# A gated MLP's first layer with seven products of parts for eight, over pairs of token blocks, on one Trainium2 core

## The chip, the core and the metric

The kernel runs on one core of a Trainium2 chip. The core has a matrix engine (TensorE, here PE), a vector engine (VectorE, DVE), an engine for activations and copies (ScalarE, ACT), a general engine (GpSimd, POOL) and a queue that issues the transfers (SyncE, SP). Only PE multiplies matrices; its results land in PSUM, eight banks of 2 KB per partition, from which DVE and ACT can read, and POOL can't in this kernel. Everything else lies in SBUF or in DRAM. The metric is the device time of one execution in microseconds (us); lower is better.

## What is computed

Decay attention over 4 batches of 8 heads, 576 positions and 64 dimensions; its output, 2304 tokens of 512 features, goes through a leaky MLP and then through a gated MLP. All in fp32:

```python
def _moe_ref(x, w_in, w_out, alpha):            # d_ff 2048
    h = x @ w_in
    g = np.maximum(h, 0.0) + alpha * np.minimum(h, 0.0)
    return (g @ w_out).astype(np.float32)

def _moe2_ref(x, w_a, w_b, w_out):              # d_ff 1536
    a = x @ w_a
    b = x @ w_b
    return (a * b @ w_out).astype(np.float32)

def reference(**kwargs):
    ...
    x = np.ascontiguousarray(attn_out.transpose(0, 2, 1, 3)).reshape(B * S, H * D)
    x = _moe_ref(x=x, **moe_kwargs)
    return _moe2_ref(x=x, **moe2_kwargs)
```

## The kernel before

**Split products.** Each fp32 number is held as a high part (rounded to the matrix engine's fp32r) and a low part, the rest. A product of two such numbers is three matmuls, high by high, high by low, low by high (`mm3`, L643 to L646). An operand that was computed is split by a cast on ACT (high) and a subtraction on POOL (low).

**Weights.** `weight` (L115 to L133) loads 512 KB by SP's queue (L123), rounds it in one ACT operation (L127) and three DVE operations (L129 to L131), casts it on ACT (L132) and subtracts on POOL (L133).

**Stages.** Attention runs up to some 366 us, with the first MLP's part a (inner blocks 0 to 6 of 16, `mlp1a`) between its steps; the rest of part a follows up to 427 us. Meanwhile the weights of inner blocks 7 to 11 are prepared, ten of them (L786 to L793). Then come two passes (L847 to L868) over six blocks of 384 tokens, with inner blocks 7 to 11 and 12 to 15: 12 matmuls for the hidden part `hb`, leaky on ACT and DVE, split on ACT and POOL (`gb`), and two inner blocks later 12 matmuls for `ya` (`passes_out`, L821 to L845). At a block's end DVE adds the running sum `yl`, loaded from DRAM. In the second pass the sum is split (`yhl`) and both parts are stored. While the passes run, weights of the next inner blocks and of the second MLP are prepared at a pace of 0.8 per inner block (L861).

**Second MLP** (L877 to L915). All its weights are resident in the end. Six token blocks of 384, twelve inner blocks each:

```python
for o, w in ((aps, W["a", fi]), (bps, W["b", fi])):
    for c in range(C):
        mm3(o[:, :n], w[:, 0, c], w[:, 1, c], yh[:, c, :n], yl[:, c, :n], c == 0, c == C - 1)
...
act.copy(asb[:, :n], aps[:, :n])
dve.tensor_tensor(asb[:, :n], bps[:, :n], asb[:, :n], op=ALU.mult)
```

That is 24 matmuls of 384 columns for `a` and `b`, a copy on ACT, the multiplication on DVE, the split into `gg`, and two inner blocks later nine matmuls of 512 columns for the output `o` (`second2`, L884), whose three banks collect all twelve inner blocks. Products rotate through four PSUM banks (`pst`, "mm"), sums through four others (`psa`, "acc"). The next block's two tiles (768 KB each) are loaded while a block runs (`load_pair`).

**What sets the order.** A framework schedules every engine's instructions by its own model of their times, from the order in which the code is written, buffer pools and priorities. Each engine then works through a fixed list; an instruction that must wait holds what stands behind it. SP's queue is such a list too.

## Time and profile before

| | |
|---|---|
| three runs | 1119.04, 1121.77, 1122.03 us, median 1121.77 |
| profiled execution | 1120.79 us, its span from first to last instruction 1119.0 us |
| mean granted clock of PE | 0.995 |
| busy share of the span | PE 95%, DVE 48%, ACT 45%, POOL 43% |
| moved by DMA | 141.18 MB, mean 126 GB/s |
| chain of work that ended last | PE 60%, DVE 4%, DMA 2%, POOL 2%, ACT 1% |

The first line is what a user sees; the profile tells of one execution only. Busy shares are means over the whole span. The chain of work that ended last is followed back from the last instruction, at each step to what released it. A wait is put down to the releaser that came last.

### The profile page before, as it was taken

Reading aid. Unit: us, or ns where it says so; the run is one execution under the profiler, and the core shown is the slowest. Engines: PE = TensorE matmul, PEld = TensorE weight load, DVE = VectorE, ACT = ScalarE, POOL = GpSimd, SP = SyncE. Lnnn points to the kernel's source line nnn. Section 1 sums busy time; section 2 is a strip of 40 time slices with the busy share of each in tenths; the row PEclk is TensorE's granted clock in tenths of the full one; section 3 lists DMA queues with packets and bytes.
Section 4 is the critical chain, followed back from the end, with each engine's and each line's share of the span. In section 5 each row is a group of like instructions: output and inputs, shape, how many; then the busy total and the mean of one; then the engine's idle time right before and its main releaser. Section 6 shows DMA issues by size and latency. Waiting matters only on the chain.

```text
span 1119.0 us, 18298 instructions
## 1 busy us (share of the span) xinstructions
PE 1064.5 (95%) x6663; PEld 1000.2 (89%) x6663; DVE 540.8 (48%) x1156; ACT 507.4 (45%) x1271; POOL 481.0 (43%) x559
## 2 busy tenths in 40 slices
PE   5989989898899998999998999999999999999997
PEld 3768988888898988999998999999999999999996
DVE  4666988888888286776577345300000000000000
ACT  5777767777677464555455543321121111111211
POOL 5445766666577355465467654311111111111111
PEclk9999999999999999999999999999999999999999
DMA  5546576776864856787778973120100100200000
GB/s 111 150 113 185 111 142 129 181 140 122 205 136 89 237 179 202 223 267 235 252 246 297 294 244 110 41 85 1 54 32 1 57 29 1 86 1 1 29 1 28
DMA packets 206093, 141.18 MB, mean 126 GB/s; under 512 B 137332, under 2 KB 195700, under 8 KB 206004
## 3 DMA queue, kind: packets, MB, share of 16 engines
q1 hardware_dynamic: 206004, 140.03, 45.0%
q8 instruction: 52, 0.85, 0.3%
q14 instruction: 37, 0.30, 0.1%
HBM read 88.30 MB, written 33.65 MB: 109 GB/s over the span
## 4 chain that ended last, share of the span: by engine, by line
PE 60%; DVE 4%; DMA 2%; POOL 2%; ACT 1%; issue 1%; SPq 0%; DVEq 0%; ACTq 0%; POOLq 0%
PE a L646 5%; PE a L645 5%; PE b L646 5%; PE b L645 5%; PE b L644 5%; PE a L644 5%; PE o L644 4%; PE o L645 4%; PE o L646 4%; PE ya L645 3%; PE ya L646 3%; PE ya L644 3%; PE hb L644 3%; PE hb L646 3%; PE hb L645 3%; DMA wr_in<-in_moe_w_in 1%
## 5 line engine op out<-in xcount | busy, mean ns | idle before, releaser
L910 DVE TENSOR_TENSOR as<-b,as 128x384 f32<-128x384 f32 x72 | 40.1, 557 | 366.4 <-PE b L646 366.4
L912 POOL TENSOR_TENSOR gg<-as,gg 128x384 fp32r<-128x384 f32 x72 | 73.7, 1023 | 330.8 <-ACT gg L911 330.8
L909 ACT COPY as<-a 128x384 f32<-128x384 f32 x72 | 34.6, 480 | 172.0 <-PE a L646 172.0
L911 ACT CAST gg<-as 128x384 fp32r<-128x384 f32 x72 | 36.9, 513 | 149.6 <-DVE as L910 149.6
L639 DVE SCALAR_TENSOR_TENSOR lt<-lu,nal,lt 128x288 f32<-128x288 f32 (+1 forms) x110 | 77.1, 701 | 52.0 <-ACT lt L638 51.6
L646 PE MATMUL a<-yh,w_a 128*128 128x384 f32 x288 | 97.2, 338 | 0.0
L646 PE MATMUL b<-yh,w_b 128*128 128x384 f32 x288 | 97.1, 337 | 0.0
L645 PE MATMUL a<-yl,w_a 128*128 128x384 f32 x288 | 97.1, 337 | 0.0
L644 PE MATMUL b<-yh,w_b 128*128 128x384 f32 x288 | 97.1, 337 | 0.0
L645 PE MATMUL b<-yl,w_b 128*128 128x384 f32 x288 | 97.1, 337 | 0.0
L644 PE MATMUL a<-yh,w_a 128*128 128x384 f32 x288 | 97.1, 337 | 0.0
L644 PE MATMUL o<-w_o,gg 128*128 128x512 f32 x216 | 84.4, 391 | 0.0
L645 PE MATMUL o<-w_o,gg 128*128 128x512 f32 x216 | 84.4, 391 | 0.0
L646 PE MATMUL o<-w_o,gg 128*128 128x512 f32 x216 | 84.2, 391 | 0.0
L355 ACT ACTIVATE s<-s,nm 128x512 f32<-128x512 f32 (+3 forms) x128 | 71.6, 560 | 15.3 <-DVE nm L354 14.1
L645 PE MATMUL ya<-gb,w_out 128*128 128x384 f32 x216 | 73.5, 340 | 1.6 <-POOL gb L641 1.6
L641 POOL TENSOR_TENSOR gb<-lt,gb 128x384 fp32r<-128x384 f32 x54 | 61.4, 1140 | 29.3 <-ACT gb L640 26.7
L646 PE MATMUL ya<-gb,w_out 128*128 128x384 f32 x216 | 73.0, 338 | 0.0
L644 PE MATMUL ya<-gb,w_out 128*128 128x384 f32 x216 | 70.7, 339 | 1.8 <-DVE yl L837 1.8
L645 PE MATMUL y<-g,w_out 128*128 128x288 f32 x224 | 66.8, 304 | 3.2 <-POOL g L641 3.0
L644 PE MATMUL h<-xh,w_in 128*128 128x288 f32 x224 | 67.3, 303 | 2.3 <-ACT lt L638 2.2
L644 PE MATMUL y<-g,w_out 128*128 128x288 f32 x224 | 65.5, 306 | 3.0 <-ACT lt L638 1.9
(185 smaller groups left out, 3150.1 us busy)
## 6 DMA issues: line engine op xcount, KB each, us to landing
yl<-ya_d SPq DMA_DIRECT2D x48, 192.0 KB
wr_in<-in_moe_w_in SPq DMA_DIRECT2D x16, 512.0 KB
wr_out<-in_moe_w_out SPq DMA_DIRECT2D x16, 512.0 KB
wr_a<-in_moe_w_a SPq DMA_DIRECT2D x12, 512.0 KB
wr_b<-in_moe_w_b SPq DMA_DIRECT2D x12, 512.0 KB
wr_o<-in_moe_w_out SPq DMA_DIRECT2D x12, 512.0 KB
qkn<-in_q SPq DMA_DIRECT2D x64, 72.0 KB
qkn<-in_k SPq DMA_DIRECT2D x64, 72.0 KB
```

The source lines that it names most:

```text
L355: act.activation(s, s, AF.Exp, bias=nm, scale=-1.0, accum_out=sm)
L639: dve.scalar_tensor_tensor(t, u, nal[:, fi:fi + 1], t, op0=ALU.mult, op1=ALU.add)
L641: pool.tensor_tensor(gl, t, f32(gh), op=ALU.subtract)
L644: pe.matmul(o, lh, rh, start=start, stop=False)
L645: pe.matmul(o, lh, rl, start=False, stop=False)
L646: pe.matmul(o, ll, rh, start=False, stop=stop)
L909: act.copy(asb[:, :n], aps[:, :n])
L910: dve.tensor_tensor(asb[:, :n], bps[:, :n], asb[:, :n], op=ALU.mult)
L911: ap_["last"] = act.copy(g[:, 0, :n], asb[:, :n]).ins
L912: pool.tensor_tensor(g[:, 1, :n], asb[:, :n], f32(g[:, 0, :n]), op=ALU.subtract)
```

## The change

The second MLP's first layer works on a pair of token blocks at once. Two token blocks (rows 1 and 2) by two halves of the 512 features (columns 1 and 2) make a 2 x 2 matrix of parts, and so do the halves of `w_a` and `w_b`. The 2 x 2 product of these takes eight products of parts; Strassen's scheme in Winograd's form takes seven, of sums of parts. A product of parts is six matmuls of 384 columns, so a pair and an inner block take 42 instead of 48.

- The sums of token parts (`pair_parts`) are made on DVE when a pair's second block leaves the second pass, and seven split tiles per pair go to DRAM: 14 `put`s a pair (a cast on ACT, a subtraction on POOL, one store), 4 behind the even and 10 behind the odd block, where there were 4 behind each block.
- `weight` for kind "b" makes four sums of weight halves on DVE and keeps five parts ("h") instead of `w_b`, with three casts and three subtractions.
- The sums of products are made on DVE, straight from PSUM.
- The twelve inner blocks are taken in three groups of four; each group goes over the three pairs (0 1 2, 2 1 0, 0 1 2), so there are 36 slots. A group's output sums go through DRAM (`po_d`): copied by ACT in the first group, added by DVE in the second and third. Weights of the next groups are loaded and prepared in the slots that `when` names.
- Seven tiles of 768 KB make a pair; `load_y` loads the next pair's tiles one by one behind the products of a turn's last slot (`leaves`), into eight buffers.
- The second layer's nine matmuls (`unit`) come twice in a slot.
- Weights in the passes come at 0.4 per inner block; the staging pool of the weights is taken ahead of the pool of x tiles; in the second pass the running sums are loaded one inner block later; at the program's start two fills move from POOL to DVE; three output buffers instead of two.

```diff
 def weight(kind, i, p, after=None):
+    x = rounded(kind, i, after)
+    if kind == "b":
+        xa = ap_["xa"]
+        s = mp["stage"].tile([128, 8, 128], F32, tag="ws", name=f"ws_{i}", bufs=1)
+        t = W["h", i] = p.tile([128, 2, 10, 128], F32R, tag="h", name=f"w_h{i}")
+        dve.tensor_tensor(s[:, 0:2], x[:, 0:2], xa[:, 0:2], op=ALU.subtract)
+        dve.tensor_tensor(s[:, 2:4], x[:, 2:4], s[:, 0:2], op=ALU.subtract)
+        dve.tensor_tensor(s[:, 4:6], x[:, 2:4], x[:, 0:2], op=ALU.subtract)
+        dve.tensor_tensor(s[:, 6:8], xa[:, 2:4], s[:, 2:4], op=ALU.subtract)
+        parts(t, slice(0, 2), x[:, 2:4])
+        parts(t, slice(2, 6), s[:, 0:4])
+        parts(t, slice(6, 10), s[:, 4:8])
+        return
...
+        dve.memset(ones, 1.0)
         for i in range(2):
...
-            fill(t[64:], 0.0)
+            dve.memset(t[64:], 0.0)
...
-            if i == 0:
-                fill(ones, 1.0)
...
+        mp["stage"] = lpool(right, "wstage2", 2, "right")
+        mp["wx"] = 3
         xp = lpool(right, "xb", 2, "right")
-        mp["stage"] = lpool(right, "wstage2", 2, "right"), C
...
-            if fi < f0 + 2:
+            if fi in (f0 + p, f0 + p + 1):
...
+        def pair_parts(blk, e, ya):
+            pair, odd = divmod(blk, 2)
+            def put(x, j, c):
+                yh = yp.tile([128, 2, TB], F32R, tag="yhl", name=f"yhl_{pair}_{j}_{c}")
+                act.copy(yh[:, 0], x)
+                pool.tensor_tensor(yh[:, 1], x, f32(yh[:, 0]), op=ALU.subtract)
+                sp.dma_start(f32(yq_d)[:, pair, j, c::2], f32(yh))
+            if not odd:
+                kept[e] = ya[e]
+                put(ya[e], 0 if e < 2 else 3, e % 2)
+            elif e >= 2:
+                c = e - 2
+                a11, a12, a21, a22 = kept[c], kept[e], ya[c], ya[e]
+                s1 = yp.tile([128, TB], F32, tag="s1", name=f"s1_{pair}_{c}", bufs=2)
+                dve.tensor_tensor(s1, a21, a22, op=ALU.add)
+                put(s1, 2, c)
...
+        visits = [0, 1, 2, 1, 0, 1, 2]
+        def load_y():
...
-                due += 0.8
+                due += 0.4
...
-        op_ = lpool(left, "os", 2)
+        op_ = lpool(left, "os", 3)
...
+            for t in range(nt):
+                acc, o = open_o[t], open_o[nt + t]
+                if g_:
+                    dve.tensor_tensor(o, acc, o, op=ALU.add)
+                else:
+                    act.copy(o, acc)
+                r0 = t0 + t * 128
+                sp.dma_start(out[r0:r0 + 128, :] if g_ == NG - 1 else po_d[g_ % 2][:, r0 // 128], o)
...
+            def both(pl, x, y, o, blk):
+                g = pl.tile([128, 2, TB], F32R, tag="g", name=f"gg_{s_}_{blk}")
+                dve.tensor_tensor(o, x, y, op=ALU.mult)
+                ap_["last"] = act.copy(g[:, 0], o).ins
+                pool.tensor_tensor(g[:, 1], o, f32(g[:, 0]), op=ALU.subtract)
+                return g
...
+            def product(j, w, c0):
+                o, y = pst.tile([128, 512], F32, tag="mm", name=f"p{j}_{s_}")[:, :TB], Y[7 * v_ + j]
+                for c in range(2):
+                    mm3(o, w[:, 0, c0 + c], w[:, 1, c0 + c], y[:, c], y[:, 2 + c], c == 0, c == 1)
+                if leaves:
+                    load_y()
+                return o
...
+            p1 = product(0, wa_, 0)
+            act.copy(ta, p1)
+            p6 = product(1, wh_, 4)
+            add(td, p6, ta)
+            p5 = product(2, wh_, 2)
+            add(tb, p5, td)
+            p2 = product(3, wa_, 2)
+            add(ta, p2, ta)
+            next_weight()
+            p3 = product(4, wh_, 0)
+            add(tc_, p3, tb)
+            ga = both(ga_, ta, tc_, tc_, 0)
+            unit(s_)
+            next_weight()
+            p7 = product(5, wh_, 6)
+            add(tb, p7, tb)
+            add(td, p7, td)
+            unit(s_)
+            next_weight()
+            p4 = product(6, wh_, 8)
+            add(td, p4, td)
+            gb = both(gp_, td, tb, td, 1)
```

**PE in the second MLP.** Before, in the third token block: `a` and `b` of inner block 4 (twelve matmuls each, three shown), then nine for the output.

```order
L644 MATMUL a_768_4_9700<-yh_768_9012,w_a4_7105 128x384 [waits Activation_49]
L645 MATMUL a_768_4_9700<-yl_768_9013,w_a4_7105 128x384
L646 MATMUL a_768_4_9700<-yh_768_9012,w_a4_7105 128x384
...
L644 MATMUL b_768_4_9701<-yh_768_9012,w_b4_7156 128x384 [waits DVE_49]
L645 MATMUL b_768_4_9701<-yl_768_9013,w_b4_7156 128x384
L646 MATMUL b_768_4_9701<-yh_768_9012,w_b4_7156 128x384
...
L644 MATMUL o_768_0_9647<-w_o2_6876,gg_768_2_9641 128x512 [waits Activation_49]
...
L644 MATMUL o_768_1_9648<-w_o2_6876,gg_768_2_9641 128x512
...
L644 MATMUL a_768_5_9741<-yh_768_9012,w_a5_7369 128x384 [waits Activation_49]
```

After, in slot 16, the first slot of a turn and group (the first matmul of each run shown; `p0` to `p6` are the products, `yq` the tiles, `o_1_...` the second layer of the turn before).

```order
L675 MATMUL p0_16_10061<-yq_21_9153,w_a4_9299 128x384 [waits DMAHW7_49,DVE_49]
...
L675 MATMUL p1_16_10069<-yq_22_9951,w_h4_9331 128x384 [waits DMAHW0_49,DVE_49]
...
L675 MATMUL p2_16_10077<-yq_23_9961,w_h4_9331 128x384 [waits DMAHW1_49,DVE_49]
...
L675 MATMUL o_1_1536_0_9916<-w_o7_9829,gg_15_0_10004 128x512 [waits Activation_49]
...
L675 MATMUL p3_16_10085<-yq_24_9971,w_a4_9299 128x384 [waits DMAHW2_49,DVE_49]
...
L675 MATMUL p4_16_10093<-yq_25_9981,w_h4_9331 128x384 [waits DMAHW4_49,Activation_49]
...
L675 MATMUL o_1_1920_0_10129<-w_o4_8700,gg_12_1_9711 128x512
...
L675 MATMUL p5_16_10120<-yq_26_10001,w_h4_9331 128x384 [waits DMAHW5_49,DVE_49]
...
L675 MATMUL o_1_1920_0_10129<-w_o5_8893,gg_13_1_9840 128x512
...
L675 MATMUL p6_16_10141<-yq_27_10024,w_h4_9331 128x384 [waits DMAHW6_49]
```

Seven runs of six matmuls stand where 48 stood, each with its own tile, and the second layer's matmuls stand between them.

**POOL where the second pass ends.** Before: the last `gb`, four splits of the running sum (`yhl`), the first `gg`.

```order
L641 TENSOR_TENSOR gb_1920_15_8338<-lt_15_8339,gb_1920_15_8338 128x384 [waits PE_49,Activation_49]
L843 TENSOR_TENSOR yhl_1920_0_8387<-yl_1_1920_0_8309,yhl_1920_0_8387 128x384 [waits DMAHW2_49,DMAHW4_49,Activation_49,Pool_49]
L843 TENSOR_TENSOR yhl_1920_1_8393<-yl_1_1920_1_8311,yhl_1920_1_8393 128x384 [waits DMAHW3_49,DMAHW0_49,Activation_49]
L843 TENSOR_TENSOR yhl_1920_2_8399<-yl_1_1920_2_8346,yhl_1920_2_8399 128x384 [waits DMAHW5_49,DMAHW2_49,Activation_49]
L843 TENSOR_TENSOR yhl_1920_3_8405<-yl_1_1920_3_8348,yhl_1920_3_8405 128x384 [waits DMAHW6_49,DMAHW4_49,Activation_49]
L912 TENSOR_TENSOR gg_0_0_8461<-as_0_0_8462,gg_0_0_8461 128x384 [waits Activation_49]
L133 TENSOR_TENSOR w_b8_8425<-wx_b8_0_8428,w_b8_8425 128x512 [waits Activation_49]
```

After, `yhl_2_...` being the last pair's puts (pair, product, half) and `w_h2` the parts of weight b of inner block 2:

```order
L1016 TENSOR_TENSOR gg_0_0_8426<-tc_0_8365,gg_0_0_8426 128x384 [waits Activation_49]
L882 TENSOR_TENSOR yhl_2_2_0_8305<-s1_2_0_8303,yhl_2_2_0_8305 128x384 [waits DMAHW0_49,Activation_49]
L882 TENSOR_TENSOR yhl_2_5_0_8310<-yl_1_1920_0_8254,yhl_2_5_0_8310 128x384 [waits DMAHW1_49,Activation_49]
L882 TENSOR_TENSOR yhl_2_1_0_8315<-yl_1_1536_0_8086,yhl_2_1_0_8315 128x384 [waits DMAHW2_49,Activation_49]
L1016 TENSOR_TENSOR gg_0_1_8457<-td_0_8366,gg_0_1_8457 128x384 [waits PE_49,Activation_49]
L882 TENSOR_TENSOR yhl_2_6_0_8319<-yl_1_1920_2_8272,yhl_2_6_0_8319 128x384 [waits DMAHW3_49,Activation_49]
L882 TENSOR_TENSOR yhl_2_4_0_8324<-yl_1_1536_2_8123,yhl_2_4_0_8324 128x384 [waits DMAHW4_49,Activation_49]
L140 TENSOR_TENSOR w_a3_8437<-wx_a3_8432,w_a3_8437 128x512 [waits Activation_49]
L882 TENSOR_TENSOR yhl_2_2_1_8331<-s1_2_1_8329,yhl_2_2_1_8331 128x384 [waits DMAHW5_49,Activation_49]
...
L1016 TENSOR_TENSOR gg_1_0_8524<-tc_1_8463,gg_1_0_8524 128x384 [waits Activation_49]
...
L1016 TENSOR_TENSOR gg_1_1_8567<-td_1_8464,gg_1_1_8567 128x384 [waits PE_49,Activation_49]
...
L140 TENSOR_TENSOR w_h2_8407<-wx_b2_8401,w_h2_8407 128x256 [waits Activation_49]
```

Puts of the last pair now stand between the first slots' `gg` and ahead of `w_h2`, and one `gg` waits in front of them.

**SP's queue near the end of the first MLP.** Before: stores of x, loads of x tiles, then the first weights of inner block 7.

```order
L560 DMA xh_d_66<-xh_3_4348 512x1x576 [waits DMAHW4_49,Activation_49]
L560 DMA xl_d_67<-xl_3_4349 512x1x576 [waits DMAHW5_49,Pool_49]
L784 DMA xh_0_5312<-xh_d_66 128x4x384 [waits DMAHW6_49,DVE_49]
L687 DMA ya_d_68<-ys_2_288_3_5289 128x288 [waits DMAHW7_49,Activation_49]
L785 DMA xl_0_5313<-xl_d_67 128x4x384 [waits DMAHW0_49,PE_49]
L123 DMA wr_in7_0_5345<-in_moe_w_in 128x4x256 [waits DMAHW1_49]
L123 DMA wr_out7_0_5381<-in_moe_w_out 128x1024 [waits DMAHW2_49]
```

After:

```order
L127 DMA wr_in7_5345<-in_moe_w_in 128x4x256 [waits DMAHW4_49,PE_49]
L127 DMA wr_out7_5381<-in_moe_w_out 128x1024 [waits DMAHW7_49,DMAHW5_49,PE_49]
L591 DMA xh_d_66<-xh_3_4349 512x1x576 [waits DMAHW6_49,Activation_49]
L591 DMA xl_d_67<-xl_3_4350 512x1x576 [waits Pool_49]
L816 DMA xh_0_5313<-xh_d_66 128x4x384 [waits DMAHW0_49,PE_49]
```

The two weights moved ahead of the stores and loads of x.

## Rows read from the trace of the kernel before

**Rows 1.** Table of stages: stretch and length, each engine's busy us, clock, DMA share, GB/s.

```profile
400.00:430.00 30.00, 24.71 (x167) 23.30 (x166) 26.19 (x30) 15.95 (x38) 17.17 (x14) 0.97 0.46 145
430.00:570.00 140.00, 139.72 (x794) 139.15 (x793) 92.96 (x133) 74.16 (x154) 70.05 (x59) 0.99 0.74 238
570.00:620.00 50.00, 46.87 (x260) 46.14 (x259) 38.66 (x47) 28.74 (x61) 36.96 (x30) 0.97 0.87 288
599.00:602.00 3.00, 3.00 (x11) 3.00 (x11) 1.65 (x4) 3.00 (x7) 3.00 (x4) 0.50 0.80 307
...
703.00:1112.00 409.00, 409.00 (x2149) 384.30 (x2148) 42.76 (x74) 75.55 (x152) 71.14 (x69) 1.00 0.08 28
```

**Rows 2.** Waits of PE from 427 us on: what waited for what, us, times, longest.

```profile
PE hb L644 <- ACT ys L686: 2.8, 1, 2.8
PE ya L644 <- DVE yl L837: 1.8, 1, 1.8
```

**Rows 3.** Timeline of PE, second MLP (start, us, instruction), then the chain's last matmuls.

```profile
690.70 0.33 PE L646 MATMUL b<-yh,w_b 128*128 128x384 f32 x1
...
691.91 0.33 PE L644 MATMUL b<-yh,w_b 128*128 128x384 f32 x1
...
1108.02 0.23 PE o L644
...
1112.10 0.24 PE o L646
```

**Rows 4.** Timeline of SP's queue in the second MLP: first load of two consecutive blocks.

```profile
805.39 0.52 SPq L785 DMA_DIRECT2D yl<-yl_d  x1
...
880.67 0.52 SPq L785 DMA_DIRECT2D yl<-yl_d  x1
```

**Rows 5.** Groups by line: instruction, count, busy us, mean ns, idle before and releaser.

```profile
L910 DVE TENSOR_TENSOR as<-b,as 128x384 f32<-128x384 f32 x72 | 40.1, 557 | 366.4 <-PE b L646 366.4
...
L641 POOL TENSOR_TENSOR gb<-lt,gb 128x384 fp32r<-128x384 f32 x54 | 61.4, 1140 | 29.3 <-ACT gb L640 26.7 <-DMA yl_d<-yhl 2.6
...
L843 POOL TENSOR_TENSOR yhl<-yl,yhl 128x384 fp32r<-128x384 f32 x24 | 27.3, 1162 | 13.6 <-ACT yhl L842 13.6
```

**Rows 6.** Timeline at the end of the first MLP, weights on DVE and POOL.

```profile
422.81 0.57 DVE L129 TENSOR_SCALAR wx_in<-wx_in 128x512 int32<-128x512 int32 x1 [0.47 <-ACT wx_in L127]
...
423.36 1.29 POOL L133 TENSOR_TENSOR w_out<-wx_out,w_out 128x512 fp32r<-128x512 f32 x1 [0.27 <-ACT w_out L132]
423.41 1.79 DVE L130 SCALAR_TENSOR_TENSOR wx_in<-wr_in,wx_in 128x512 int32<-128x512 int32 x1
...
425.24 0.69 DVE L131 SCALAR_TENSOR_TENSOR wx_in<-wr_in,wx_in 128x512 int32<-128x512 int32 x1
```

**Rows 7.** Timeline of PE behind the wait at 427.48.

```profile
429.02 0.52 PE L644 MATMUL hb<-xh,w_in 128*128 128x384 f32 x1
429.34 0.52 PE L645 MATMUL hb<-xl,w_in 128*128 128x384 f32 x1
```

**Rows 8.** Table of single microseconds while a pair of tiles is loaded.

```profile
807.00:808.00 1.00, 1.00 (x7) 0.92 (x6) 0.00 (x0) 0.00 (x0) 0.84 (x1) 1.00 0.83 184
808.00:809.00 1.00, 1.00 (x7) 1.00 (x6) 0.00 (x0) 0.00 (x0) 0.00 (x0) 1.00 1.01 373
```

**Rows 9.** Chain that ended last, end of the first MLP.

```profile
380.71 10.85 DMA wr_in<-in_moe_w_in
```

**Rows 10.** Timeline of the start.

```profile
7.45 1.35 DVE L170 TENSOR_TENSOR_SCAN rows<-rows 64x576 f32<-64x576 f32 x1 [3.74 <-POOL rows L144]
...
10.45 0.64 SPq L176 DMA_DIRECT2D N<-rows  x1
```

**Rows 11.** Timeline of the end.

```profile
1112.97 3.25 SPq L897 DMA_DIRECT2D out<-os  x3
1115.17 0.69 DVE L896 COPY os<-o 128x512 f32<-128x512 f32 x1 [7.85 <-DMA out<-os]
```

More of the change, by code (lines that the diff above doesn't have):

```diff
@@ L96, in decay_attention_then_two_mlps @@
     ya_d = dram.tile([128, C, T], F32, name="ya_d")
-    yh_d = dram.tile([128, C, T], F32R, name="yh_d")
-    yl_d = dram.tile([128, C, T], F32R, name="yl_d")
+    yq_d = dram.tile([128, NPAIR, 7, 4, TB], F32R, name="yq_d")
+    po_d = [dram.tile([128, T // 128, DM], F32, name=f"po_d{i}") for i in range(2)]
     cum_d = [dram.tile([B * NP, 4, SP + S], F32, name=f"cum_d{j}") for j in range(2)]
@@ new lines, in parts @@
+    def parts(t, o, x):
+        act.copy(t[:, 0, o], x)
+        pool.tensor_tensor(t[:, 1, o], x, f32(t[:, 0, o]), op=ALU.subtract)
+    def weight(kind, i, p, after=None):
+        x = rounded(kind, i, after)
[11 more added lines that the diff above has]
+            return
+        if kind == "a":
+            ap_["xa"] = x
+        t = W[kind, i] = p.tile([128, 2, C, 128], F32R, tag="w", name=f"w_{kind}{i}")
+        parts(t, slice(0, C), x)
@@ L866, in decay_attention_then_two_mlps @@
                     w2ctx.close()
-                    w4 = lpool(right, "w4", W2, "right")
-                    todo += [u + (w4,) for u in mlp2[:W2]]
+                    mp["yq"] = lpool(right, "yq", 4, "right")
+                    ga_ = lpool(right, "ga", 3, "right")
+                if p and t0 in (3 * TB, 5 * TB) and fi == f0:
+                    for _ in range(4 if t0 == 3 * TB else 2):
+                        load_y()
+        load_y()
+        while todo:
+            weight(*todo.pop(0), ap_["last"])
@@ new lines, in decay_attention_then_two_mlps @@
+        hp.append(lpool(left, "h2", FG // 2))
+        op_ = lpool(left, "os", 3)
+        turns = [(g_, pair) for g_ in range(NG) for pair in range(NPAIR)[::(1, -1)[g_ % 2]]]
+        slots = [(i, fi) for i in range(len(turns)) for fi in range(FG)]
+        when = {0: [("b", 2), ("a", 3)], 1: [("b", 3), ("o", 3)]}
+        for g_ in range(1, NG):
+            s_ = (g_ * NPAIR - 1) * FG
+            for fi in range(FG):
+                f_ = g_ * FG + fi
+                last = fi == FG - 1
+                when.setdefault(s_ + fi + 1 + last, []).extend([("a", f_), ("b", f_)] + [("o", f_)] * last)
+                if not last:
+                    when.setdefault(s_ - 5 + 2 * fi, []).append(("o", f_))
@@ L900, in decay_attention_then_two_mlps, with next_weight @@
+        v_ = 0
+        for s_, (i, fi) in enumerate(slots):
+            g_, pair = turns[i]
+            if i and not fi and turns[i - 1][1] != pair:
+                v_ += 1
+            leaves = fi == FG - 1 and i + 1 < len(turns) and turns[i + 1][1] != pair
+            f_ = g_ * FG + fi
+            todo = [u + ((hp[u[1] % FG // 2] if u[0] == "b" else w1),) for u in when.get(s_, [])]
+            def next_weight():
                 if todo:
                     weight(*todo.pop(0), ap_["last"])
-                aps = pst.tile([128, 512], F32, tag="mm", name=f"a_{t0}_{fi}")
@@ L903, in decay_attention_then_two_mlps @@
-                bps = pst.tile([128, 512], F32, tag="mm", name=f"b_{t0}_{fi}")
-                for o, w in ((aps, W["a", fi]), (bps, W["b", fi])):
-                    for c in range(C):
-                        mm3(o[:, :n], w[:, 0, c], w[:, 1, c], yh[:, c, :n], yl[:, c, :n], c == 0, c == C - 1)
-                g = gp_.tile([128, 2, TB], F32R, tag="g", name=f"gg_{t0}_{fi}")
-                asb = tp.tile([128, TB], F32, tag="lt", name=f"as_{t0}_{fi}")
-                act.copy(asb[:, :n], aps[:, :n])
@@ L910, in decay_attention_then_two_mlps @@
-                dve.tensor_tensor(asb[:, :n], bps[:, :n], asb[:, :n], op=ALU.mult)
-                ap_["last"] = act.copy(g[:, 0, :n], asb[:, :n]).ins
-                pool.tensor_tensor(g[:, 1, :n], asb[:, :n], f32(g[:, 0, :n]), op=ALU.subtract)
-                later(partial(second2, t0, n, fi, g, st))
-        while behind:
-            behind.pop(0)()
+            def both(pl, x, y, o, blk):
[4 more added lines that the diff above has]
+                return g
@@ L918 @@
+            next_weight()
[7 more added lines that the diff above has]
+            gb = both(gp_, td, tb, td, 1)
+            units[i, 0, fi], units[i, 1, fi] = (s_, ga), (s_, gb)
+        while units:
+            unit(len(slots))
 _INS = ["q", "k", "v", "f", "moe_w_in", "moe_w_out", "moe_alpha", "moe2_w_a", "moe2_w_b", "moe2_w_out"]
```

149 lines of the change are left out of this document (84 added, 65 removed).

## The prediction, made before the changed kernel ran

> **What bounds the kernel now.** I read the page first, then the table of stages, then PE's waits, and only then single instructions. The page's busy shares mix stages with different limits, so the table of stages decides [rows 1]: from 703 to 1112 us PE is busy for all 409.00 us at granted clock 1.00, while DVE has work for 42.76 us and ACT and POOL for some 75 each. That stretch is the second MLP, and no wait of PE lies in it [rows 2]. There a matmul taken out is time taken out, as long as DVE, POOL and the transfers still keep up. Earlier it differs: 400:430 has PE busy for 24.71 of 30 us, 570:620 for 46.87 of 50, both at clock 0.97 [rows 1]; the two longest of PE's waits behind 427 us, 2.8 and 1.8 us [rows 2], lie in these stretches.
>
> **First layer: the term that carries the forecast.** In the second MLP seven matmuls of 384 columns start between 690.70 and 691.91 us [rows 3], 0.173 us apart; matmuls of 512 columns start 0.227 us apart (18 from 1108.02 to 1112.10) [rows 3]. One token block of twelve inner blocks lasts from 805.39 to 880.67, 75.28 us [rows 4], 6.273 us each; with nine of 512 columns that leaves 24 x 0.176. I take 0.176, since it comes from a whole block. Before: 72 x 6.273 = 451.7 us. After: 36 slots of seven products x 6 matmuls x 0.176 = 7.40 us and two units of nine x 0.2275 = 4.10 us, so 11.49 us each, 413.7 us. The order on PE has the same 216 rows fewer. **-38.0 us**, if PE stays fed.
>
> **Steady slots.** Each slot has nine DVE operations instead of two multiplications. At 557 ns [rows 5] that is 5.0 us of 11.5; POOL's two subtractions and ACT's copy and casts fill less. Four banks hold the products, so PE can run three products ahead, about 3 us, against one DVE operation of 0.56 us that frees a bank. I price it at 0. What is new: the multiplication now reads two SBUF tiles, where before one input lay in PSUM. DVE's operation on two SBUF tiles took 0.69 us at 425.24 and 1.79 us at 423.41, when POOL's subtraction of 423.36 ran beside it [rows 6]. So a 0.56 us operation may take some 1.4 us beside POOL; in a steady slot there is room for that.
>
> The Trainium skill (GPSIMD Engine Reference, Specifications) says that GpSimd shares its SBUF interfaces with VectorE and that instructions with two SBUF inputs contend. The rows agree. By the rule every sum of parts and every multiplication beside a subtraction pays, so the start and the changes of group below would stand at the bad ends that rows 6 give them, and the sum at 1093 instead of 1083; that speaks against this change and is a part of rival 1. The bounds themselves come from the rows alone.
>
> **Start of the second MLP.** Before, DVE had four sums of the passes there and POOL four subtractions. The order now puts ten DVE sums, the last pair's ten puts (cast, subtraction, store) and w_a3, w_h2, w_h3 into the first three slots. POOL stands at gg_0_0 first: 78 matmuls after the first product (48 are the last ones of the passes) x 0.176 = 13.7 us, then two DVE operations and a cast, so 15.4. Behind it wait ten puts at 1.16 [rows 5] = 11.6, gg_0_0 and three more like it at 1.1 to 1.2 = 4.5, w_a3 1.3 [rows 6]: 32.8 us; then the three pieces of w_h2, 0.7 + 1.3 + 1.3, to 36. PE asks for w_h2's first piece after 150 matmuls of 384 and 24 of 512 columns, at 31.9, and for the rest within 2 us. DVE has about 25 us of work for those slots, and up to 9 more if the ten sums each meet POOL [rows 6]. Hence a stall of 2 to 10 us; a slow clock may follow: after the 2.8 us wait 13 matmuls started 0.32 us apart instead of 0.176 [rows 7], 1.9 us, the pitch of the clock's lower level, 1.2 GHz (granted clock 0.50, as again from 599 to 602 behind the 1.8 us wait [rows 1]). In the kernel before the same place has no wait [rows 2], so the lower end is 0. **+6** (0 to +12).
>
> **Two changes of group.** In four slots each, DVE gets weights a and b: three operations each (0.57 + 0.69 + 0.69, or 3.0 us with one beside POOL [rows 6]) and four sums of half a tile, about 0.37 each from the 0.69 us row. With a half of them beside POOL 5.0 + 2 x 2.35 + 1.5 = 11.2 us, with all some 13.5, against PE's 11.5. The three products of slack take most of it. **+2** (0 to +8).
>
> **Six changes of pair.** In the last slot of a turn each product frees a tile for the next pair, 768 KB each. The first store is free 1.1 us into the slot, the sixth tile is wanted 10.4 us into the next one, 21.9 us in all. A load issued at 805.39 [rows 4] ran at half rate by 807 and at 373 GB/s from 808 [rows 8], so 2 us pass first, once, since the loads follow each other without a gap; then a tile takes 2.1 us, six 12.6, so all arrive. With partial sums and a weight between them (1.3 to 2.1 MB) and at the rate of a busy mixed stretch (145 GB/s at share 0.46, so 315 when full [rows 1]) it is 6.0 to 6.8 MB in 19.1 to 21.7 us, plus 3.1: 22.2 to 24.8 against 21.9, if all of it came first. **+2** (0 to +17, six times 2.9 us).
>
> The Trainium skill (DMA: Bandwidth & Descriptors, the anatomy of one DMA on the SWDGE path) fits a transfer as about 2.0 us plus its bytes at 436 GB/s. If a tile paid that alone, as an estimate from that page, it would take 3.8 us, each switch would come some 2 us late, and the sum would be 1093. The rows of the load at 805 us disagree, so the sum goes without it.
>
> **The passes.** PE is idle for 0.3 us in 430:570 and 3.1 in 570:620, and clock 0.97 in the latter [rows 1] costs another 1.5; with 2 us of slow start [rows 7] that makes about 7 us lost there now, with weights on DVE when the wait for its sum came. The pace of weights halves (0.4 a slot instead of 0.8), which takes work from DVE just where it was late. Against it: ten puts now come behind each odd block, where POOL's g of the pass stands in the same queue (1.14 us each [rows 5]), and the running sums are read later, behind tiles of 768 KB in SP's queue. A g late by three puts (3.5 us) at two bursts would cost 7 and the clock. **0** (-5 to +8).
>
> **End of the first MLP.** The stretch loses 5.3 us at 400:430 [rows 1] because the weights' first load starts at 380.71, behind stores and loads of x, and takes 10.85 us [rows 9]; what follows is one chain of weights on DVE up to the 2.8 us wait. Now two weights are asked for ahead of these. That takes perhaps 4 to 6 us off the chain. The x tiles, on the other hand, come that much later; PE has the rest of part a meanwhile. **-5** (0 to -7).
>
> **Both ends.** At the start the scan at 7.45 us waited 3.74 us for POOL's fill of ones [rows 10]; on DVE it is ready earlier, but SP still has loads to issue up to 9.0, so the row store moves from 10.45 to about 9 and the first scores come earlier with it. **-1.5** (0 to -2.5). At the end DVE's copy at 1115.17 waited for a store from one of two buffers [rows 11]; with three, a 0.69 us sum and a store of about 2.2 us follow the last matmul: 3.6 us instead of 6.7. **-3**.
>
> **Sum.** -38.0 - 1.5 - 5 + 0 + 6 + 2 + 2 - 3 = -37.5 us. The profiled execution took 1120.8 us (span 1119.0 and 1.8 around it), 1.0 under the median of the three runs, 1121.8; I sum against it: **1083 us**.
>
> **Rivals.** (1) *The feeders eat a third of it.* Every start, group and pair change runs at the bad end of its own row: +10, +6, +8 and passes +4 instead of +6, +2, +2 and 0, so 1101; half of that gives 1092. For it: rows 6, and the thin margin of the pair changes; against: three products of slack. (2) *Slower: the pair changes starve.* One SP queue carries tiles, partial sums and weights, each issue in order. Six switches must lose the 39.5 us that the other terms give, 6.6 each; 1.9 of that would be the slow clock [rows 7], so 4.7 us idle: six tiles in 23.5 us instead of 18.8, 201 GB/s. A stretch of 400:430 moved 145 GB/s, but with engines at a share of 0.46 [rows 1], so by demand. At 170 GB/s (4.6 us a tile) a switch loses 8.8 + 1.9, six 64, and the kernel takes 1120.8 - 39.5 + 64 = 1145. (3) *Everything fits.* No stall at the start, in groups or pairs, and the passes get 3 back: 1083 - 10 - 3 = 1070. (4) *It doesn't do what it says*: the matmuls are not fewer. The order shows that they are.
>
> **How the numbers follow.** Forecast 1077 to 1090: 0.50. Rival 1, 1090 to 1115: 0.30. Rival 3, 1064 to 1077: 0.13. Rival 2, above 1117: 0.06; rival 4: 0.01. The range that holds 8 in 10 leaves out half of rival 3 and the far part of rival 1 with rival 2: **1070 to 1102**. A step of 0.3% (3.4 us) is about what can be told from no change. Faster 0.92, same 0.03, slower 0.05.
>
> **What would show it.** In the second MLP slots should start 11.5 us apart at clock 1.00, with about 6,440 PE records instead of 6,663 on the page. Waits of PE on POOL's w_h2 in the third slot, on DVE's wx parts at the group changes and on DMA tiles in the first slots of a turn would be the three prices; none of them means rival 3. If the last of these waits exceeds 4 us at each switch, rival 2 is right. If 400:430 still loses 5 us, the term of the first MLP's end is wrong; if PE waits for gb in the second pass behind puts, that of the passes. After the last matmul there should be 3 to 4 us. The forecast fails as a whole if DVE's operations on two SBUF tiles run at 1.4 us throughout and PE waits for banks in every slot.

## The result, and the profile after

The changed kernel takes **1089.1 us** in the median of four runs (1086.7 to 1092.87) against 1121.33 for the kernel before: ratio **0.9719** (95% interval 0.9687 to 0.9751), 32 us faster. A second set of four runs gave 1088.11 (1087.23 to 1089.23), ratio 0.9711 (0.9696 to 0.9725); it is the base of the experiments below and is called "after, again". The profiled execution of the first set is its slowest, 1092.87 us; the profiled one of the second, 1088.12, is near the median.

The page of after, busy time of each engine:

```profile
PE 1032.3 (95%) x6447; PEld 964.7 (88%) x6447; DVE 734.2 (67%) x1518; ACT 508.7 (47%) x1278; POOL 521.0 (48%) x598
```

PE has 216 records fewer than before, as many as the scheme saves. The table of stages of after (columns as in [rows 1]):

```profile
400.00:430.00 30.00, 26.33 (x184) 25.29 (x183) 23.70 (x29) 16.47 (x39) 17.77 (x14) 0.98 0.46 143
430.00:570.00 140.00, 140.00 (x797) 140.00 (x796) 64.31 (x105) 63.73 (x135) 54.13 (x51) 0.99 0.64 205
570.00:620.00 50.00, 48.97 (x282) 48.68 (x281) 29.38 (x41) 26.73 (x58) 34.77 (x32) 1.00 0.77 266
620.00:660.00 40.00, 40.00 (x233) 40.00 (x232) 23.17 (x34) 18.73 (x42) 26.46 (x26) 1.00 1.00 364
660.00:700.00 40.00, 31.10 (x145) 27.60 (x144) 33.71 (x51) 14.84 (x31) 28.99 (x25) 0.91 0.58 196
...
750.00:1050.00 300.00, 298.32 (x1552) 277.15 (x1551) 206.20 (x354) 74.74 (x147) 98.56 (x88) 1.00 0.50 176
```

The second MLP is PE-bound again (298.32 of 300 us at clock 1.00, last row), but the stretch in which it starts, 660:700, has PE idle for 8.9 of 40 us at a mean clock of 0.91, while DVE is busy for 33.71. The waits of PE in after from 364 us on (what waited for what, us, times, longest):

```profile
PE p L675 <- DVE td L1032: 3.6, 4, 1.9
PE o L675 <- ACT gg L1015: 3.4, 1, 3.4
PE hb L675 <- ACT ys L717: 2.9, 1, 2.9
...
PE p L675 <- ACT w_h L139: 1.4, 1, 1.4
...
PE p L675 <- DVE lt L1032: 1.0, 1, 1.0
```

`hb` is the wait of [rows 2] at the end of the first MLP, unchanged. All others shown, bar three short ones of `td` (1.7 us together), lie between 673 and 696. There is none for a tile of a pair (`yq`), and the wait of `ya` for DVE's `yl` in [rows 2] is gone. PE's own landmarks in after (start, us, instruction):

```profile
11.89 2.05 PE L369 MATMUL sc<-N 128*128 128x512 f32 x2 [4.72 <-DMA N<-rows]
...
374.82 0.19 PE L544 MATMUL pv<-PT_r,vs 128*128 128x64 f16 x1
...
427.54 0.44 PE L675 MATMUL hb<-xh,w_in 128*128 128x384 f32 x1 [2.88 <-ACT ys L717]
...
1086.95 0.39 PE L677 MATMUL o<-w_o,gg 128*128 128x512 f32 x1
```

They are the first scores, attention's last matmul, the first matmul of the passes and the last matmul of all. In the kernel before, attention's last matmul starts at 373.20, not at some 366 us. Between it and the passes every kernel here has the same 357 matmuls of the first MLP. With the same landmarks of each kernel, each by its start, length of each stage in us:

| stage | before | after | after, again | i9 (below) |
|---|---|---|---|---|
| to the first scores | 13.0 | 11.9 | 11.9 | 11.9 |
| to attention's last matmul | 360.2 | 362.9 | 359.3 | 359.4 |
| rest of the first MLP | 54.3 | 52.7 | 52.2 | 52.3 |
| the passes | 233.5 | 228.8 | 228.2 | 226.1 |
| second MLP | 451.4 | 430.6 | 430.6 | 423.2 |
| from the last matmul on | 6.6 | 4.1 | 4.1 | 4.1 |

The second MLP is counted from the last matmul of the passes, less 0.176 us for each of its own matmuls that stand ahead of that one (11, 14, 14, 17). Between before and after, again: 1.1 + 0.9 + 2.1 + 5.3 + 20.8 + 2.5 = 32.7 us. The first three of these are not firm: two executions of the same changed kernel lie 4 us apart in the second and third row together.

**The slots.** 1552 matmuls in 298.32 busy us, 60 to a slot, are 11.53 us a slot, so 36 slots need 415.1 us. The second MLP took 15.5 more. How much of it belongs to the start can be read from 660:700: with the start's stall gone (experiment e1 below) PE has 213 matmuls there, in after 145, in after, again, 141. The 68 to 72 missing ones at 11.53/60 = 0.192 us are **13.1 to 13.8 us**, idle time and slow clock together.

**What PE waits for at the start.** Timeline of DVE, POOL, PE and ACT in after:

```profile
676.01 1.16 DVE L896 TENSOR_TENSOR yl<-s,yl 128x384 f32<-128x384 f32 x1
...
676.71 1.31 POOL L882 TENSOR_TENSOR yhl<-s,yhl 128x384 fp32r<-128x384 f32 x1
...
677.55 1.02 DVE L134 SCALAR_TENSOR_TENSOR wx_b<-wr_b,wx_b 128x512 int32<-128x512 int32 x1
678.50 1.34 DVE L899 TENSOR_TENSOR yl<-yl,yl 128x384 f32<-128x384 f32 x1
679.76 0.54 DVE L1014 TENSOR_TENSOR tc<-lt,tc 128x384 f32<-128x384 f32 x1
...
680.90 0.51 PE L675 MATMUL o<-w_o,gg 128*128 128x512 f32 x1 [3.44 <-ACT gg L1015]
...
686.60 0.41 ACT L139 CAST w_h<-wx_b 128x256 fp32r<-128x256 f32 x1 [1.85 <-POOL yhl L882]
...
689.47 1.10 DVE L133 TENSOR_SCALAR wx_o<-wx_o 128x512 int32<-128x512 int32 x1 [5.69 <-ACT wx_o L131]
```

The last pair's sums (L896, L899: two tiles in SBUF) take 1.16 and 1.34 us beside POOL's subtractions of the puts, an operation on a weight's data (L134) stands between them, and the multiplication `tc` of the slot stands behind all three; PE gets its `gg` 3.44 us late. Later ACT's cast for w_h2 waits for POOL's `yhl`, in whose memory the weight lies. The chain of work in after, again, there (start, us, what):

```profile
678.87 1.33 POOL yhl L882
680.22 3.59 DMA yq_d<-yhl
683.81 0.02 issue
683.83 0.04 ACTq L139
...
684.22 0.68 ACT wx_o L131
```

This L139 is the fourth cast there, the first of w_h3 (the three of w_h2 stand ahead of it): it has to wait for the store of a put out of the memory that w_h3 takes, and behind it in ACT's queue stands `wx_o`, for which DVE waits (the 5.69 us above).

### The profile page after: what moved, and what is told of

Its sections match the earlier page's. It is cut to its first block, busy times and chain, and to the rows that moved or that the text cites. A ratio compares the mean times of both kernels' runs of the same rounds, so it can differ in the third digit from the quotient of the medians.

```text
span 1091.1 us, 18574 instructions
## 1 busy us (share of the span) xinstructions
PE 1032.3 (95%) x6447; PEld 964.7 (88%) x6447; DVE 734.2 (67%) x1518; ACT 508.7 (47%) x1278; POOL 521.0 (48%) x598
## 4 chain that ended last, share of the span: by engine, by line
PE 55%; DVE 7%; POOL 2%; DMA 2%; issue 2%; ACT 2%; ACTq 0%; POOLq 0%; DVEq 0%; SPq 0%
PE p L675 7%; PE p L677 7%; PE p L676 7%; PE o L677 4%; PE o L676 4%; PE o L675 4%; PE ya L675 3%; PE ya L676 3%; PE ya L677 3%; PE hb L675 3%; PE hb L677 3%; PE hb L676 3%; DMA yq_d<-yhl 1%; POOL yhl L882 1%; DVE lt L670 1%
## 5 line engine op out<-in xcount | busy, mean ns | idle before, releaser
L675 PE MATMUL p<-yq,w_h 128*128 128x384 f32 x360 | 122.3, 340 | 4.3 <-DVE td L1032 2.2
L676 PE MATMUL p<-yq,w_h 128*128 128x384 f32 x360 | 121.8, 338 | 0.0
L677 PE MATMUL p<-yq,w_h 128*128 128x384 f32 x360 | 121.4, 338 | 0.0
L1016 POOL TENSOR_TENSOR gg<-tc,gg 128x384 fp32r<-128x384 f32 x36 | 36.6, 1017 | 113.7 <-ACT gg L1015 103.5
L672 POOL TENSOR_TENSOR gb<-lt,gb 128x384 fp32r<-128x384 f32 x54 | 56.3, 1044 | 64.8 <-ACT gb L671 64.8
L1016 POOL TENSOR_TENSOR gg<-td,gg 128x384 fp32r<-128x384 f32 x36 | 37.6, 1044 | 93.3 <-ACT gg L1015 87.6
L1015 ACT CAST gg<-tc 128x384 fp32r<-128x384 f32 x36 | 18.5, 514 | 124.2 <-DVE tc L1014 123.7
L675 PEld LDWEIGHTS p<-yq,w_h 128*128 128x128 f32 x360 | 67.9, 188 | 9.1 <-issue 2.2
L676 PE MATMUL y<-g,w_out 128*128 128x288 f32 x224 | 68.0, 308 | 3.5 <-POOL g L672 3.5
L676 PEld LDWEIGHTS p<-yq,w_h 128*128 128x128 f32 x360 | 67.8, 188 | 3.5
L677 PE MATMUL y<-g,w_out 128*128 128x288 f32 x224 | 66.9, 305 | 2.3 <-POOL w_out L140 2.3
L672 POOL TENSOR_TENSOR g<-lt,g 128x288 fp32r<-128x288 f32 x56 | 54.9, 984 | 27.3 <-ACT g L671 25.4
L675 PE MATMUL y<-g,w_out 128*128 128x288 f32 x224 | 66.5, 311 | 1.5 <-ACT g L671 1.4
```

The lines of the kernel that those rows point to most:

```text
L672: pool.tensor_tensor(gl, t, f32(gh), op=ALU.subtract)
L675: pe.matmul(o, lh, rh, start=start, stop=False)
L676: pe.matmul(o, lh, rl, start=False, stop=False)
L677: pe.matmul(o, ll, rh, start=False, stop=stop)
L1015: ap_["last"] = act.copy(g[:, 0], o).ins
L1016: pool.tensor_tensor(g[:, 1], o, f32(g[:, 0]), op=ALU.subtract)
```

## Experiments

Each is an edit of the changed kernel, of which the main lines are shown; ratios are against the kernel before on the same chip. "Matmuls" is PE's count in 660:700.

| run | median us | ratio [interval] | matmuls, clock |
|---|---|---|---|
| after, again | 1088.11 | 0.9711 [0.9696, 0.9725] | 141, 0.91 |
| e1 no last puts | 1074.16 | 0.9581 [0.9564, 0.9597] | 213, 1.00 |
| e2 no weights at the start | 1075.86 | 0.9600 [0.9586, 0.9614] | 208, 1.00 |
| i1 weights a slot later | 1086.25 | 0.9692 [0.9676, 0.9708] | 153, 0.87 |
| e4 puts without sums | 1083.42 | 0.9672 [0.9645, 0.9699] | 154, 0.91 |
| e5 pace of weights 0.8 | 1089.10 | 0.9721 [0.9697, 0.9745] | 132, 0.83 |
| e6 fills and pool as before | 1086.49 (one run) | | 144, 0.91 |
| i7 w_h2 in its own place | 1087.64 | 0.9708 [0.9688, 0.9729] | 182, 0.96 |
| i8 i7, weights a slot later | 1083.00 | 0.9665 [0.9637, 0.9693] | 190, 1.00 |
| i9 w_h2 and w_a3 in the passes | 1079.53 | 0.9636 [0.9622, 0.9651] | 193, 1.00 |
| i10 w_h2 in the passes | 1082.56 | 0.9656 [0.9630, 0.9682] | 191, 0.96 |
| i11 i9, fills on POOL | 1077.67 | 0.9615 [0.9599, 0.9630] | 192, 1.00 |

**After, again**, unchanged, as the base.

> The changed kernel once more, unchanged, as the base for what runs beside it. Expected: 1086 to 1093 us; PE idle in its third to fifth slot of the second MLP (some 9 us between the first product and 700 us in the first profile), and no wait of PE on a tile at the changes of pair.

It came out within the first set's runs.

**e1: no sums and puts behind the last pair's second block** (products p0 and p3 read the last pair's own tiles, the other five those of the pair before).

```
-            elif e >= 2:
+            elif e >= 2 and pair < NPAIR - 1:
...
```

> The last pair's ten puts and the sums for them are left out; five of its seven tiles are read from the pair before, so the output isn't the reference's. Theory (the loss of 12.5 us at the start of the second MLP comes from the last pair's puts and the weights of inner blocks 2 and 3 meeting on DVE, ACT and POOL in the first slots): without the puts the weights alone fit, the loss falls to 3 or less, 1080 us. Rival (weights alone: they stand in front of sums on DVE and wait for their load): 7 or more of the loss stay, 1086 us or more.

```profile
660.00:700.00 40.00, 40.00 (x213) 37.68 (x212) 31.26 (x50) 14.17 (x27) 19.73 (x18) 1.00 0.64 232
```

PE never stops in the row of e1 that answers to 660:700, and the kernel is 14.0 us faster: all of the start's loss, with the weights still in their place. By the landmarks its second MLP lasts 417.1 us, 13.5 less than in after, again.

**e2: no weights at the start** (w_h2, w_h3, w_a3, w_o3 are not prepared, and older ones read).

```
-        when = {0: [("b", 2), ("a", 3)], 1: [("b", 3), ("o", 3)]}
+        when = {}
...
```

> The weights of inner blocks 2 and 3 that are prepared in the first two slots are left out and those of 0 and 1 used again, so the output isn't the reference's. Theory (puts and weights together): the puts alone fit within PE's time for the first three slots, the loss falls from 12.5 to 4 or less, 1080 us. Rival (puts alone, a ring of four buffers behind slow stores): 8 or more of the loss stay, 1086 us or more.

12.3 us faster with all puts there (second MLP 417.2 us). Either load alone fits beside the slots; together they don't. So neither is "the" cause: it is that both come in the same 30 us. Both runs also take out transfers, ten stores here and four loads of weights there, so they don't tell at which engine or queue the two loads meet.

**i1: the same weights later.**

```
-        when = {0: [("b", 2), ("a", 3)], 1: [("b", 3), ("o", 3)]}
+        when = {0: [("b", 2)], 1: [("a", 3)], 2: [("b", 3), ("o", 3)]}
```

> Weights b3 and o3 are prepared in the third slot instead of the first two; nothing else changes. Theory: DVE waited 5.7 us at o3's first operation with the parts of b3 and a sum for PE behind it; that wait leaves the first slots and 2 to 5 us of the loss go, 1085 us. Rival: b3 is then late for the fourth slot and PE waits there instead, 1089 us or more.

1.9 us of 14 (w_a3 moved by a slot too). A wait of 3.9 us for `gg` stays and the one for w_h2 is 1.9: what is late is w_h2 and the puts, which did not move.

**e4: the last pair's puts without their sums on DVE** (cast, subtraction and store stay, of tiles that are not summed).

```
-                dve.tensor_tensor(s1, a21, a22, op=ALU.add)
-                put(s1, 2, c)
+                put(a21, 2, c)
...
```

> The last pair's ten puts stay, but the ten sums that DVE makes for them are left out (the puts take the tiles as they are, so the output isn't the reference's). It asks which engine carries the loss at the start of the second MLP. If DVE does (its sums took 1.2 to 1.4 us beside POOL instead of 0.55, some 10 us in the first two slots): most of the 13.5 us goes, 1078 us or less. If the way of the puts does (ACT's cast, POOL's subtraction, a store from a ring of four buffers, and w_h2 behind the last of them): less than a half goes, 1082 us or more.

The edit leaves out eight sums, four for each half, not ten. The time fell by 4.7 us, with runs from 2.3 to 7.5 under after, again. The wait for `gg` fell to 1.7, but PE now waits 4.3 us for w_h2. (PE's 154 matmuls are those of e4's slowest run.) So DVE's sums are a part of the loss, about a third by the medians; the rest stays without them, and the wait for w_h2 puts it on the way of the puts, casts, subtractions and stores, and of the weight behind them. How it is shared among these was not tried.

**e5: weights in the passes at the old pace.**

```
-                due += 0.4
+                due += 0.8
```

> Weights in the two passes come at 0.8 per inner block again instead of 0.4, the same fourteen. Theory (the passes are 5 us shorter than before because DVE has fewer weights when sums for PE are late): 3 to 5 us come back while the fourteen last, 1091 to 1093 us. Rival (the passes are shorter for another reason: sums loaded later, eight buffers for them): no change, 1088 us.

```profile
570.00:620.00 50.00, 50.00 (x290) 49.82 (x289) 23.95 (x32) 24.40 (x54) 31.58 (x30) 1.00 0.74 252
```

No difference in the time; PE is busy for 139.75 us in 430:570 and 50.00 in 570:620. At the old pace the weights, sixteen of them, are all done in the first pass (the last one begins on DVE at 510 us), so this run shows that the pace costs nothing there. It doesn't show that the passes' gain has nothing to do with weights: in 570:620, where the kernel before lost its time, DVE has 23.95 us of work here, 29.38 in after and 38.66 before.

**e6: the fills of ones and N on POOL, and x's pool ahead of the weights' stage pool, as before.**

> Two small parts of the change undone in one kernel, at places that don't touch: the fills of the start are back on POOL, and the staging pool of the weights comes after the pool of x tiles again. Read from the trace, beside 11.9, 362.3 and 423.4 us of the changed kernel: first scores about 1 us later (13.0), the end of attention 1 to 2 us later if the head's gain lasts, and the same if it is lost on the way; from there to the passes' first matmul about 63.5 us instead of 61.1 if the order of the two pools makes that gain, 61 if it doesn't. Time 1090 to 1092, or 1088 if neither counts.

The sum barely moved, but the stages did. The first scores came at 10.13 us instead of 11.91; that went into i11. Behind attention's last matmul (it starts at 371.24 in after, again, not at the 362.3 of the expectation) the first MLP took 55.9 us, where the other twelve profiles with the change's pools have 52.2 to 52.7. But the stretch ahead of it was shorter by as much: from the first scores to the passes e6 takes 413.2 us, and i11, with the same fills and the change's pools, 413.2 too. So the order of the pools moves work from one side of attention's end to the other, and no gain of it is shown.

**i7: w_h2 gets memory of its own** and is prepared in the second pass; the tiles of the pairs get seven buffers instead of eight.

```
-        todo += [("o", 2, w1), ("a", 2, w1)]
+        todo += [("o", 2, w1), ("a", 2, w1), ("b", 2, None)]
...
-                    mp["yq"] = lpool(right, "yq", 4, "right")
+                    mp["yq"] = lpool(right, "yq", 3, "right")
+                    hp.append(lpool(right, "h2", 1, "right"))
...
-        when = {0: [("b", 2), ("a", 3)], 1: [("b", 3), ("o", 3)]}
+        when = {0: [("a", 3)], 1: [("b", 3)], 2: [("o", 3)]}
...
```

> w_h2 gets a place of its own and is prepared within the passes; for its room seven tile buffers serve instead of eight, and a3, b3, o3 are prepared in slots 0, 1, 2. Theory: without w_h2 behind the puts and with fewer weights in the first slots, 8 to 11 of the 13.5 us go, 1077 to 1080 us. If seven buffers are too few at the changes of pair, PE waits for tiles there, up to 3 us at each, 1090 us or more.

A miss: the start gains (182 matmuls), the total doesn't. Its waits of PE:

```profile
PE p L675 <- DMA yq<-yq_d: 3.2, 2, 2.7
...
PE ya L675 <- DVE yl L868: 1.7, 2, 1.1
```

The weight, now beside the second pass's puts (from 604 us on, amid ten puts at 591 to 608), brings back the wait of `ya` for DVE that before had, and PE's busy time in 570:620 falls to 47.91; and a tile comes 2.7 us late, with 242 matmuls in 700:750 instead of 265. The seven buffers don't do it: i9 below has them too, and no such wait.

**i8: i7 with its other weights a slot later.**

```
-        when = {0: [("a", 3)], 1: [("b", 3)], 2: [("o", 3)]}
+        when = {1: [("a", 3)], 2: [("b", 3)], 3: [("o", 3)]}
```

> As i7_h2_own_place, with a3, b3, o3 one slot later (1, 2, 3). Theory: the first two slots are then free of weights but one, 10 to 12 of the 13.5 us go, 1076 to 1078 us. Rival: b3 comes late for the fourth slot and PE waits 3 to 5 us there, 1080 us or more.

5.1 us under after, again. Its chain of work at the wait for a tile that is left:

```profile
693.32 0.61 DVE wx_o L135
...
693.99 0.33 SPq L127
...
694.37 8.37 DMA yq<-yq_d
...
702.88 0.41 PE p L675
```

The tile's load stands in SP's queue behind the load of a weight's raw data, which can be issued only when DVE has left the stage buffer (`wx_o`, L135). In i7 the 2.7 us have the same chain.

**i9 and i10: w_h2 so early that it meets the second pass's first block and not its puts** (pace 0.455); i9, whose lines stand here, has w_a3 in the second pass's last block too, i10 leaves it in the second MLP's second slot.

```
-                due += 0.4
+                due += 0.455
...
+                if p and t0 == 5 * TB and fi == f0 + 1:
+                    weight("a", 3, w1, ap_["last"])
...
+        when = {1: [("b", 3)], 2: [("o", 3)]}
```

> As i8, but b2 is prepared in the second pass's first block, where there are no puts, a3 in its last block ahead of its puts, b3 and o3 in slots 1 and 2. Theory (weights cost PE where they meet puts): the 1.4 us wait that i8 showed in the second pass behind its weights goes, and so do most of the 3.3 us left at the start, 1077 to 1080 us. Rival: a3 beside the transfers of the last block (340 GB/s there) delays its puts, 1082 us or more.

> As i8, with the one difference that b2 is prepared in the second pass's first block. Theory: the wait of PE on a sum in the second pass (1.4 us and its slow clock) goes, 1080 to 1082 us. Rival (the wait there doesn't come from the weight): it stays, 1083 us.

```profile
570.00:620.00 50.00, 50.00 (x289) 49.76 (x288) 33.16 (x43) 26.81 (x60) 38.37 (x34) 1.00 0.83 292
...
660.00:700.00 40.00, 37.86 (x193) 34.13 (x194) 33.14 (x50) 13.88 (x29) 24.25 (x21) 1.00 0.74 266
```

In i9's rows of the table of stages the passes stay full and the clock is 1.00: 8.6 us under after, again. i10 is 5.5 under it; its interval overlaps i9's, so what w_a3's place is worth stays uncertain. Against i8, from which it differs only in where w_h2 comes (from 583 us on), i10 has no wait for `yl` and PE busy for all 50 us of 570:620 instead of 48.39, but the time is the same within the runs (1082.56 and 1083.00): the place beside the puts is shown as a wait, not as time. PE's 20 missing matmuls in i9 are 3.8 us that remain of the start there; by the landmarks its second MLP is 6.1 us longer than e1's, so some 2 more lie elsewhere.

**i11: i9 with the fills back on POOL**, POOL's order of its other memsets as in the change.

```
-        dve.memset(ones, 1.0)
...
-            dve.memset(t[64:], 0.0)
+            fill(t[64:], 0.0)
...
+            if i == 0:
+                fill(ones, 1.0)
```

> The kernel with w_h2 and w_a3 in the passes, and beside it the fills of ones and of the two tiles N back on POOL, as the kernel before has them, while the change's order of POOL's other memsets (those of vs and sr behind the fills) stays. It tells apart which of the two edits of the start brings the earlier first scores. If it is the order of the memsets, DVE's two fills of 1.07 us and the one of 0.54 only stand ahead of DVE's own first operation, the first scores come at about 10.1 us instead of 11.9, as in the run that had them on POOL, and the kernel takes 1079.5 - 1.8 = 1077.7 us. If the moved fills bring it, the first scores come at 13 us and the time is about 1080.6. If attention takes the gain back (its pipeline waits on something else later), the first scores come at 10.1 and the time stays at 1079.5.

The first scores come at 10.13 us, so the order of POOL's memsets brings what the start gains, and the fills on DVE give 1.8 us of it back. The time, 1077.67, agrees with the 1.8 arriving at the end, but the intervals of i9 and i11 overlap, and in i11's profiled execution (its slowest) attention's last matmul starts only 0.5 us before i9's: whether the whole gain arrives is open. By its median it is the fastest version here and beats both kernels.

## Why the prediction was right, and where its steps were not

The time came 6 us above the forecast, inside the range and inside the forecast's own case, near its end towards rival 1. The mechanism was the one named: fewer matmuls on a PE that is fed, less what the start of the second MLP costs. By the terms below the sum is -36.3 - 1.1 - 0.9 (attention, not forecast) - 2.1 - 5.3 + 13.5 + 2 - 2.5 = -32.7 us, as by the landmarks. That it came so near is in part luck: the start cost 7.5 us more than its term, the passes gave 5.3 that were forecast as 0, and the two nearly cancel.

**First layer (-38.0): -36.3.** 415.1 us for 36 slots against 451.4. The slot is 11.53, not 11.49: matmuls of 512 columns in the middle of the second MLP start 0.230 us apart, not 0.2275, which came from the quiet end of [rows 3].

```profile
801.49 0.39 PE L675 MATMUL o<-w_o,gg 128*128 128x512 f32 x1
...
802.41 0.40 PE L676 MATMUL o<-w_o,gg 128*128 128x512 f32 x1
```

In after's timeline of PE these two are four apart, 0.92 us.

**Steady slots (0): right.** Groups of DVE in after from 700 us on:

```profile
L1032 DVE TENSOR_TENSOR td<-p,td 128x384 f32<-128x384 f32 x66 | 36.4, 551 | 37.0 <-PE p L677 36.8
...
L1014 DVE TENSOR_TENSOR tc<-lt,tc 128x384 f32<-128x384 f32 x33 | 21.8, 662 | 0.8
L1014 DVE TENSOR_TENSOR td<-td,lu 128x384 f32<-128x384 f32 x33 | 18.3, 556 | 0.9
```

Two lines of the timeline of DVE and POOL there:

```profile
783.82 1.29 POOL L140 TENSOR_TENSOR w_a<-wx_a,w_a 128x512 fp32r<-128x512 f32 x1 [2.01 <-ACT w_a L139]
784.05 1.47 DVE L1014 TENSOR_TENSOR tc<-lt,tc 128x384 f32<-128x384 f32 x1
```

The multiplication of two SBUF tiles costs 0.56 to 0.66 us on the mean: POOL rarely runs beside it, and DVE waits for PE. Of the 66, 59 took 0.54 to 0.56 us; the three slowest, 1.40 to 1.47, lie at the first change of group, with a subtraction of POOL beside them for about 1 us, as in the last two lines. At the start such operations cost 1.16 to 1.38 beside POOL. The rule of the Trainium skill (GPSIMD Engine Reference, Specifications), that instructions with two SBUF inputs contend with GpSimd, agrees with all of these. The sum of 1093 that the prediction drew from it was 4 us too high: the start was worse than its bad end, the changes of group were not.

**Start of the second MLP (+6): +13.5, the step that failed.** The prediction took one queue for the price, POOL's up to w_h2, and gave DVE's 25 us and up to 9 more no wait of their own. w_h2 was ready at 690.3 us, 42 behind the first product at 648.2, not 36. But of the 8.9 us that PE stands there, the waits listed above give w_h2 only 1.4; 7.1 are for sums and a `gg` that come late from DVE. Four things were left out. The memory of w_h2 is that of the put buffers, so it waits for their last reader. The four put buffers come free only with the stores (ACT waits 6.2 us for these between 640 and 692), in part while the transfers are at share 1.00 (620:660). DVE's work for puts and weights stands ahead of the slots' sums. And w_o3, which the prediction doesn't count, is prepared there too: its three operations on DVE and w_h3's sums stand ahead of the `td` for which PE waits 1.9 us. Each of e1 and e2 alone takes the loss away, which shows the meeting; e4 puts about a third on DVE's sums. The slow clock followed as forecast: 0.91 in 660:700.

**Groups and pairs (+2, +2): about +2 together.** Behind 700 us PE's waits are 1.7 us for `td`, as at 800.33 and 803.29 at a change of group; no wait for a tile in after. Rival 2 falls. In the working for the groups a half of the operations beside POOL gives 2 x 2.5 and not 2 x 2.35, so 11.5 us and not 11.2; the term doesn't hang on it. From the fit on the other page of the Trainium skill (DMA: Bandwidth & Descriptors, the anatomy of one DMA on the SWDGE path) the prediction estimated 2 us at each switch; no switch shows that. The page states the fit for transfers that GpSimd issues, and SyncE issues these.

**Passes (0): -5.3, just outside its bounds.** PE is busy for 49 to 50 of 50 us in 570:620 where before had 46.87. The reason given, less work on DVE where its sum was late, agrees with DVE's 29.38 us in 570:620 against 38.66 before. What i7 and i8 show, against i10, is that one weight beside the second pass's puts from 604 us on is enough to bring back the wait for `yl`; before, weights came up to 612 us, now the last begins at 594. So the place counts more than the pace, and the term's price was wrong for what stood against it: the feared delay of `gb` behind the puts came to 1.0 us once.

**End of the first MLP (-5): -2.1, and not firm.** From the first scores to the passes before took 414.5 us, after 415.7, after, again 411.5, so what the earlier weights gain isn't told from the scatter of single executions, and e6 shows no gain of the pools. In 400:430 PE still loses 3.7 us in after and 3.3 in after, again. Timeline in after, again:

```profile
418.39 0.33 SPq L127 DMA_DIRECT2D wr_out<-in_moe_w_out  x1
...
421.92 0.66 ACT L131 ACTIVATE wx_out<-wr_out 128x512 f32<-128x512 f32 x1 [2.39 <-DMA wr_out<-in_moe_w_out]
...
423.00 0.69 ACT L717 COPY ys<-y 128x288 f32<-128x288 f32 x2
...
423.44 0.44 PE L675 MATMUL hb<-xh,w_in 128*128 128x384 f32 x1 [2.66 <-ACT ys L717]
```

Asking for weights earlier doesn't help where ACT's copy `ys`, which frees PE's bank, stands behind ACT's operation on the next weight, and that waits for its load. I followed the chain of weights and not ACT's queue.

**Both ends (-1.5, -3): -1.1 and -2.5.** The end went as told: one sum and one store behind the last matmul.

```profile
1087.37 0.69 DVE L993 TENSOR_TENSOR os<-o,os 128x512 f32<-128x512 f32 x1 [0.97 <-PE o L677]
```

At the start the size was near, the reason wrong: i11 and e6 show that the fills on DVE cost 1.8 us, and that the order of POOL's memsets gained more than that. In [rows 10] the scan waited for POOL's fill of ones because memsets of `vs` had gone ahead of it. The last of these and the fill of ones in before, then that fill in i11:

```profile
5.34 0.25 POOL L248 MEMSET vs<- 64x192 f32 x1
...
6.83 0.58 POOL L144 MEMSET rows<- 64x576 f32 x1
```

```profile
3.81 0.75 POOL L172 MEMSET rows<- 64x576 f32 x1
```

## What to carry to other kernels

Where two stages meet, the old one's last stores and the new one's first weights use the same three engines; price them as one load, with each buffer's last reader and each store that frees one, and not queue by queue. When both loads fit alone, move one of them into a stretch with idle feeders, and look at what it meets there (beside the previous stage's puts in i7 and i8 it brought back a wait of 1.4 to 1.7 us; i7 gained nothing, i9 8.6 us). When an engine waits for a short copy, look at what stands ahead of that copy in its engine's queue before moving loads forward.
